# Folding two forward transforms and normalising rows block by block in a fused long-convolution and token-mixing kernel

## The chip, the cores and the metric

The kernel runs on one core of a Trainium2 chip. The metric is the device time of one execution in microseconds (us); lower is better. "Span" is the time from the first to the last instruction in the profile; in these kernels the device time is the span plus about 1.8 to 2.4 us. TensorE multiplies matrices, VectorE (DVE in the profile), ScalarE (ACT) and GpSimd (POOL) do the rest, SyncE (SP) issues most transfers. GpSimd issues the others, in particular those that add to their destination.

## The reference, cut to what matters

```python
def _A_ref(q, k, v, shift_k, ssm_k, ssm_D):          # S = 2048 rows, D = 640
    k_shift = sum of 4 shifted copies of k, each times a tap of shift_k
    kv = k_shift * v
    y  = irfft(rfft(kv, 4096) * rfft(ssm_k, 4096))[:2048]     # long convolution
    return q * (y + kv * ssm_D)

def _B_ref(x, w1, b1, w2, b2):
    h = layernorm(x)                                  # over D
    return w2^T @ gelu(w1^T @ h + b1) + b2            # mixes the S rows

x = A_q;  g = sigmoid((x * gate_w).sum(-1))
result = g * _A_ref(x, ...) + (1 - g) * _B_ref(x, ...)        # as the kernel combines them
```

The kernel does the Fourier transforms as matrix products with sine tables (`FTB` forward, `GTB` inverse). There are two pairs of forward transforms: of the filter (`wT`, two halves) and of `kv` (`vkv0` and `kv1`). Between transforms VectorE runs "mixings", additions and subtractions that combine four partial spectra.

## The kernel before

The kernel holds its own list scheduler. It gives every operation an assumed duration, simulates the engines, and emits each engine's instructions in the order that this simulation found. Semaphore waits are then added from real data dependencies.

```python
def dma(o, i, nbytes, stream="SP", prio=None, sem=None, rate=320.0, chain=False, **kw):
    ...  # the scheduler assumes nbytes / rate for a transfer

def k_turn(hk):                       # one block of keys: a copy on VectorE, then a transposing transfer
    o, i = kp[hk % 2], kn[hk % 2]
    ...  # VectorE copy kp <- kn
    dma(KT[hk // 2][:, :, c0:c0 + 128], o[:, :, :], 128 * 5120, rate=170.0, transpose=True, chain=True)

def ln_apply():                       # after the statistics of all 16 row tiles
    ts("POOL", sd[:, :], mv[:, :, 1], 1e-5, None, ALU.add)
    tt("POOL", rstd[:, :], sd[:, :], V(cst, 1, [[0, 16]]), ALU.pow)
    tt("POOL", sd[:, :], sd[:, :], rstd[:, :], ALU.mult)
    for t in range(16):
        ...  # VectorE: X[t] = (X[t] - mean) * rstd

def v1mix(Wh, Ws, Vh, Vs):            # two transfers that ADD reversed spectra to their destination
    for i in range(2):
        dma(V(Vh, ...), V(Wh, ...), 128 * 5120 * 2, stream="POOL", prio=0, accum=True)
v1mix(C[0], 2, C[1], 2)
v1mix(SS, 0, C[0], 0)
```

`KT` (transposed keys) feeds the shift products on TensorE, which give `ksh`. VectorE multiplies that with `v` into `vkv`, and the transform of `vkv` follows.

Of the kernel before, what the change touches and what calls it, by code (L numbers as in the profile page):

```python
# [11 lines left out]
I32 = mybir.dt.int32  # L12
ACT = mybir.ActivationFunctionType
# [5 lines left out]
class _Tracker:  # L19
# [31 lines left out]
    def regions(self, ap):  # L51
# [10 lines left out]
        pstride, pcount = apl[0]  # L62
        if pcount > 1:
            assert pstride == rowsize, (name, apl, rowsize)
        p0 = off // rowsize
# [187 lines left out]
    def dma(self, stream, out_ap, in_ap, semname, transpose=False, noncontig=False, accum=False):  # L253
        reads = [in_ap] + ([out_ap] if accum else [])
        writes = [out_ap]
        acc = self.pre(stream, reads, writes)
        engobj = self.eng[stream]
        sem = self.dma_sems[semname]
        if transpose:
            ins = engobj.dma_start_transpose(out_ap, in_ap)  # L260
        elif accum:
            ins = engobj.dma_start(out_ap, in_ap, accum_op=ALU.add, max_dma_last_dim=2560)  # L262
        elif noncontig:
            with self.nc.allow_non_contiguous_dma(reason="tiny"):
                ins = engobj.dma_start(out_ap, in_ap)
        else:
            ins = engobj.dma_start(out_ap, in_ap)  # L267
        ins.then_inc(sem, 16)
        self.dma_cnt[semname] += 16
        v = self.dma_cnt[semname]  # L270
        self.dma_hist[(semname, v)] = dict(self.known[stream])
        src = ("dma", semname, v)
        for reg, mode in acc:
            self.add_record(reg, mode, src)
        return v
# [229 lines left out]
def _build(nc, A_q, A_k, A_v, A_shift_k, A_ssm_k, A_ssm_D, B_x, B_w1, B_b1, B_w2, B_b2, gate_w, out):  # L505
# [10 lines left out]
    with ExitStack() as es:  # L516
# [38 lines left out]
        cw = alloc("cw", [128, NG, 7], BF16)  # L555
        m32 = alloc("m32", [128, 32], BF16)
        cc = alloc("cc", [128, 28], F32)
        stats = alloc("stats", [128, 16, 12], F32)
# [11 lines left out]
        FTB = alloc("FTB", [128, 4, 2, 2, 2, 128], BF16)  # L570
# [7 lines left out]
        acol = alloc("acol", [128, 2, 4], I32, at=base_of(SS))  # L578
        brow = alloc("brow", [128, 2, 128], I32, at=base_of(SS) + 64)
        dif = alloc("dif", [128, 128], I32, at=base_of(SS) + 64 + 1024)  # L580
        dif2 = alloc("dif2", [128, 32], I32, at=base_of(SS) + 64 + 1536)
        KT = [alloc(f"KT{i}", [128, NG, KTW], BF16) for i in range(2)]
        gq = [alloc(f"gq{i}", [128, 2, D], BF16, at=base_of(GTB) + 2560 * i) for i in range(3)]
        ssm = alloc("ssm", [128, ND, S], BF16, at=base_of(C[3]))
        wT = alloc("wT", [128, 4, 4, D], BF16, at=base_of(C[2]))
# [7 lines left out]
        pint = alloc("pint", [128, 4, 2, 2, 256], I32, at=base_of(ring[1]))  # L593
# [88 lines left out]
        def dma(o, i, nbytes, stream="SP", prio=None, sem=None, rate=320.0, chain=False, **kw):  # L682
# [5 lines left out]
            rd = [i] + ([o] if kw.get("accum") else [])  # L688
# [19 lines left out]
        def ssm_load(hk):  # L708
            dma(ssm[:, :, 512 * hk:512 * hk + 512], dr(A_ssm_k, 512 * hk, [[S, 128], [128 * S, ND], [1, 512]]), 128 * ND * 1024, chain=True)
# [4 lines left out]
        def w1_load(c, hk):  # L714
            dma(ring[c % 2][:, 4 * hk:4 * hk + 4, :], dr(B_w1, 512 * hk * F + 512 * c, [[4 * F, 128], [F, 4], [1, 512]]), 128 * 4096, chain=True)

        def k_load(hk):
            dma(kn[hk % 2][:, :, :], dr(A_k, 512 * hk * D, [[4 * D, 128], [1, 4 * D]]), 128 * 5120, chain=True)

        def k_turn(hk):  # L720
# [4 lines left out]
            c0 = 16 + 128 * (hk % 2)  # L725
            dma(KT[hk // 2][:, :, c0:c0 + 128], o[:, :, :], 128 * 5120, rate=170.0, transpose=True, chain=True)

        def v_load(hk):
            dst = vkv0[:, hk, :, :] if hk < 2 else v1[:, hk - 2, :, :]
            dma(dst, dr(A_v, 512 * hk * D, [[4 * D, 128], [1, 4 * D]]), 128 * 5120, chain=True)  # L730
# [8 lines left out]
        for hk in range(2):  # L739
            ssm_load(hk)  # L740
# [5 lines left out]
        dma(gwb[:, :], dr(gate_w, 0, [[0, 128], [1, D]]), 128 * 1280, chain=True)  # L746
        for hk in range(1, 4):
            x_load(hk)
        ssm_load(2)
        ssm_load(3)  # L750

# [5 lines left out]
        iota(acol[:, :, :], [[512, 2], [1, 4]], 0, 4)  # L757
        iota(brow[:, :, :], [[2, 2], [4, 128]], 1, 0)
        iota(dif2[:, :], [[1, 32]], 128, -1)
        ts("DVE", ident[:, :], dif[:, :], 0.0, None, ALU.is_equal)  # L760
        memset("POOL", cw[:, :, :], 0.0)
        ro, ri = rows[0:20, 3, :].rearrange("g (j q c) -> g j q c", j=4, q=4), V(rows, 0, [[1, 4], [0, 4], [4, 32]], pn=20)
        SC.add("POOL", 1.3, lambda s: T.op("POOL", lambda e: e.tensor_copy(ro, ri), [ri], [ro]), [ri], [ro], name="taps")
        PORD = (0, 2, 1, 3)
        for p in PORD:
            pv = pint[:, p, :, 1, :]
            tt("DVE", pv, V(acol, p, [[4, 2], [0, 256]]), V(brow, 0, [[0, 2], [1, 256]]), ALU.mult, mode=1)
            ts("DVE", pint[:, p, :, 0, :], pv, 1024.0, None, ALU.add, mode=2)
            pa = pint[:, p, :, :, :].rearrange("q a b c -> q (a b c)")
            ts("DVE", pa, pa, 4095, None, ALU.bitwise_and, mode=2)  # L770
            act(FTB[:, p, :, :, :, :].rearrange("q a b c d -> q (a b c d)"), pa, ACT.Sin, bias=cst[:, 0:1],
                scale=-(2.0 * math.pi / 4096.0) * (1.0 - 1e-6), name="sin")

        for hk in range(2):
            k_load(hk)
        for hk in range(4):
            w1_load(0, hk)

# [15 lines left out]
        def transp(h, p, kt):  # L794
            vt = _VT("cv")
            items = []
            hk = 2 * h + kt
            dfold = hk == 0 and p == 0
# [3 lines left out]
            for db in range(ND):  # L802
                items.append(((lambda s, db=db: s[:, db * 128:db * 128 + 128]),
                              V(ssm, db * S + 512 * hk + p, [[4, 128]]), ident[:, :], not dfold, True))
            mms(vt, items, name="wtr")
            act(wT[:, hk, p, :], full, ACT.Copy, vt=vt, name="wT")

        def fwd(src, h, p, dst, slot, scale, name, neg=lambda c, k2: False):
            for k2 in range(2):
                for c in range(2):  # L810
                    vt = _VT("cv")
                    items = []
                    for kt in range(2):
                        for ci in range(2):
                            items.append((chk(ci), FTB[:, p, kt, c, k2, :], src(kt, p, ci), kt == 0, kt == 1))
                    mms(vt, items, name=name)
                    o = dst[:, slot, 2 * c + k2, :].rearrange("p (a b) -> p a b", a=2)
                    sc = -scale if neg(c, k2) else scale
                    kw = {} if sc == 1.0 else {"scale": sc}
                    act(o, two, ACT.Copy, vt=vt, name=name + "e", **kw)  # L820

        def mixing(R, Th, Ts, fine=False, conj=False):
            def sl(h, s, n=1):
                return V(h, s * SL, [[1, n * SL]])
# [3 lines left out]
            for i, n in (((0, 1), (1, 1)) if fine else ((0, 2),)):  # L828
                tt("DVE", sl(Th, Ts + i, n), sl(R, i, n), sl(R, 2 + i, n), ALU.add)
                tt("DVE", sl(R, i, n), sl(R, i, n), sl(R, 2 + i, n), ALU.subtract)  # L830
            tt("DVE", sl(R, 2), sl(Th, Ts), sl(Th, Ts + 1), ALU.add)
            tt("DVE", sl(R, 3), sl(Th, Ts), sl(Th, Ts + 1), ALU.subtract)
# [16 lines left out]
        def ln_apply():  # L849
            ts("POOL", sd[:, :], mv[:, :, 1], 1e-5, None, ALU.add)  # L850
            tt("POOL", rstd[:, :], sd[:, :], V(cst, 1, [[0, 16]]), ALU.pow)
            tt("POOL", sd[:, :], sd[:, :], rstd[:, :], ALU.mult)
            for t in range(16):
# [3 lines left out]
        srcW = lambda h: (lambda kt, p, ci: wT[:, 2 * h + kt, p, 320 * ci:320 * ci + 320])  # L857
        for h in range(2):
            for p in PORD:
                for kt in range(2):  # L860
                    transp(h, p, kt)
            for p in PORD:
                fwd(srcW(h), h, p, C[h], p, 1.0 / 1024.0, "W", (lambda c, k2: k2 == 1) if h == 0 else (lambda c, k2: c == 1))
            if h == 0:
# [3 lines left out]
                ln_apply()  # L868
                for g0 in (0, 10):
                    tt("POOL", KF[:, g0:g0 + 10, :, :], V(cw, 7 * g0, [[7, 10], [1, 7], [0, 32]]), V(m32, 0, [[0, 10], [0, 7], [1, 32]]), ALU.mult)  # L870
                for hk in range(2):
                    k_turn(hk)
                mixing(C[0], SS, 0, fine=True)
            else:
                mixing(C[1], C[0], 0, conj=True)

        memset("POOL", KT[0][:, :, 15:16], 0.0)
        for hk in range(2):
            v_load(hk)
        for hk in range(2, 4):  # L880
            k_load(hk)
        for hk in range(2, 4):
            v_load(hk)
        for hk in range(2, 4):
            k_turn(hk)
        for hk in range(4):
            w1_load(1, hk)

        def v1mix(Wh, Ws, Vh, Vs):
            for i in range(2):  # L890
                dma(V(Vh, (Vs + i) * SL, [[1280, 2], [1, 1280]]), V(Wh, (Ws + i) * SL + 1280, [[-1280, 2], [1, 1280]]),
                    128 * 5120 * 2, stream="POOL", prio=0, accum=True)

        v1mix(C[0], 2, C[1], 2)
        v1mix(SS, 0, C[0], 0)

        def kv(hk):
            h, kt = hk // 2, hk % 2
            kb = ksh[hk % 2]
            for g0, ng in ((0, 8), (8, 8), (16, 4)):  # L900
                vt = _VT("cv")
                items = []
                for b in range(ng):
                    g = g0 + b
                    c0 = 16 + 128 * kt
                    items.append(((lambda s, b=b: s[:, 128 * b:128 * b + 128]), KT[h][:, g, c0:c0 + 128],
                                  KF[:, g, 0:4, :].rearrange("p a b -> p (a b)"), True, False))
                    items.append(((lambda s, b=b: s[:, 128 * b:128 * b + 96]), KT[h][:, g, c0 - 1:c0 + 127],
# [244 lines left out]
```

## Time and profile before

| | before |
|---|---|
| device time, median | 192.68 us (192.67 to 192.70) |
| span | 190.9 us |
| TensorE busy | 177.4 us (93%) |
| VectorE busy | 170.3 us (89%) |
| first forward transform of the filter / of kv starts | 14.29 / 50.28 us |

The next lines are from the page of the kernel before: busy time by engine, and TensorE's busy share and granted clock, in tenths, in 40 slices of the span.

```profile
PE 177.4 (93%) x1403; PEld 130.5 (68%) x1403; DVE 170.3 (89%) x195; ACT 116.4 (61%) x187; POOL 33.0 (17%) x29
...
PE   0749989999799999999999999999999999999993
...
PEclk9999999999999999999999999999999999999999
```

TensorE works almost without a break after the first quarter. (The trace's records of the granted clock begin at 16.3 us in this run, so the 9s of `PEclk` before that say nothing.) To see how much it loses even while "busy", I took the start of every matmul from the trace and subtracted from each interval what that matmul takes when nothing holds it: 0.1357 us for 320 columns, 0.0557 us for 128 and 0.0425 us for 96, the spacings of its unhindered stretches. The remainder is lost time. By this estimate, the kernel before has 169.1 us of matmul work and loses 18.6 us: 12.5 us by 17.1 us, 5.2 us from there to 62 us, and 0.8 us after that.

This is the timeline of SyncE's queue in the kernel before (start, length of the issue, source line, transfer, count):

```profile
22.42 10.61 SPq L260 DMA_TRANSPOSE KT<-kp  x2
...
48.19 6.34 SPq L260 DMA_TRANSPOSE KT<-kp  x2
```

And this is GpSimd's timeline, with the adding transfers:

```profile
57.02 2.64 POOL L262 DMA_DIRECT2D C<-C  x2 [19.65 <-DVE C L617]
61.34 2.43 POOL L262 DMA_DIRECT2D C<-SS  x2 [1.68 <-DVE C L617]
```

From the view of the tile `KT` in the kernel before, the time from issue to landing of the four transposes:

```profile
DMA to landing us min/median/max: 4.9/5.0/9.7
```

The last transpose is issued at 51.35 us and has landed by 56.3 us. The adding transfers begin at 57.02 us. The two kinds do not meet, but nothing in the program sees to that.

### The profile page before, as it was taken

To read this page: it belongs to the slowest core of one execution; us is meant where nothing else is said; L and a number is where in the kernel's file an instruction comes from. 1 tells how busy PE (TensorE), PEld (TensorE's weight loads), DVE (VectorE), ACT (ScalarE), POOL (GpSimd) and SP (SyncE) were. 2 spreads that over 40 slices of the span, in tenths; PEclk is the share of its full clock that TensorE was granted. 3 is DMA by queue.
4 is the path that set the end of the run, shared out by engine and by line. 5 is a ranking of instruction groups with operands and counts; after the bars stand their busy time and mean duration, and the time that the engine had idled before them with its cause. 6 is when DMAs were issued, how large, how long until landed. Compare 5 with 4: busy or idle time off the path is not lost.

```text
span 190.9 us, 3358 instructions
## 1 busy us (share of the span) xinstructions
PE 177.4 (93%) x1403; PEld 130.5 (68%) x1403; DVE 170.3 (89%) x195; ACT 116.4 (61%) x187; POOL 33.0 (17%) x29
## 2 busy tenths in 40 slices
PE   0749989999799999999999999999999999999993
PEld 0536555678566976767777777888888777886782
DVE  7999967999999799999999969999999958999451
ACT  4799997889599999998411221131322467516632
POOL 2619563600006300010012102250000000000000
PEclk9999999999999999999999999999999999999999
DMA  5999999993799999994368914999947903210222
GB/s 155 327 412 378 372 238 230 307 407 136 136 181 306 250 232 306 272 329 96 59 138 251 231 27 138 272 208 195 263 136 224 367 18 137 72 69 2 72 103 103
DMA packets 37296, 38.93 MB, mean 204 GB/s; under 512 B 15644, under 2 KB 32673, under 8 KB 37281
## 3 DMA queue, kind: packets, MB, share of 16 engines
q1 hardware_dynamic: 34464, 32.15, 54.7%
q0 software_dynamic: 2752, 6.55, 18.6%
q8 instruction: 11, 0.18, 0.4%
q14 instruction: 5, 0.03, 0.0%
q10 hardware_dynamic: 64, 0.01, 0.0%
HBM read 25.87 MB, written 2.62 MB: 149 GB/s over the span
## 4 chain that ended last, share of the span: by engine, by line
PE 71%; DVE 19%; DMA 4%; POOL 2%; issue 2%; SPq 0%; ACT 0%; DVEq 0%
PE pp L293 71%; DVE stats L845 6%; DMA X<-in_A_q_dram 4%; DVE X L628 3%; DVE SS L617 3%; DVE C L617 2%; DVE kp L724 2%; POOL rstd L617 2%; DVE vkv L617 1%; DVE mv L847 1%; POOL sd L627 1%; SPq L267 0%; ACT O L655 0%; DVE O L617 0%; DVEq L187 0%
## 5 line engine op out<-in xcount | busy, mean ns | idle before, releaser
L293 PE MATMUL pp<-X,ring 128*128 128x320 bf16 x384 | 54.0, 299 | 0.1
L293 PE MATMUL pp<-GT,W 128*128 128x320 bf16 x384 | 52.8, 299 | 0.0
L617 DVE TENSOR_TENSOR C<-C 128x2560 bf16<-128x2560 bf16 (+1 forms) x28 | 48.9, 1769 | 1.2 <-ACT C L655 1.1
L293 PEld LDWEIGHTS pp<-GT,W 128*128 128x128 bf16 x384 | 43.5, 113 | 8.9 <-ACT cgb L655 0.2
L293 PEld LDWEIGHTS pp<-X,ring 128*128 128x128 bf16 x384 | 37.1, 98 | 15.4 <-DVE X L628 0.7
L655 ACT ACTIVATE C<-pp 128x640 bf16<-128x640 f32 x64 | 39.6, 741 | 4.4 <-PE pp L293 4.3
L655 ACT ACTIVATE O<-pp,c,omg 128x640 bf16<-128x640 f32 (+1 forms) x17 | 14.5, 853 | 32.9 <-PE pp L293 32.9
L655 ACT ACTIVATE GT<-pp,cc 128x640 bf16<-128x640 f32 x12 | 9.6, 797 | 22.1 <-PE pp L293 21.9
L617 DVE TENSOR_TENSOR tm<-C,C 128x2560 bf16<-128x2560 bf16 (+2 forms) x12 | 20.2, 1708 | 1.9 <-DMA C<-tm 1.9
L293 PE MATMUL pp<-wT,FTB 128*128 128x320 bf16 x128 | 19.6, 310 | 0.6 <-ACT wT L655 0.4
L655 ACT ACTIVATE cgb<-pp,gg 128x640 bf16<-128x640 f32 x16 | 12.7, 793 | 7.7 <-PE pp L293 7.7
L293 PEld LDWEIGHTS pp<-wT,FTB 128*128 128x128 bf16 x128 | 11.5, 101 | 8.0 <-ACT C L655 2.3
L617 DVE TENSOR_TENSOR C<-tm 128x2560 bf16<-128x2560 bf16 (+1 forms) x12 | 15.0, 1263 | 0.1
L293 PE MATMUL pp<-ident,ssm 128*128 128x128 bf16 x80 | 8.8, 265 | 6.6 <-DMA ssm<-in_A_ssm_k_dram 5.3
L262 POOL DMA_DIRECT2D C<-C x6 | 7.5, 1407 | 36.0 <-DVE C L617 36.0
L845 DVE BATCH_NORM_STATS2 stats<-X 128x6 f32<-128x320 bf16 x32 | 13.4, 463 | 0.3 <-DMA X<-in_A_q_dram 0.3
L293 PE MATMUL pp<-C,GTB 128*128 128x320 bf16 x96 | 13.6, 299 | 0.0
L293 PEld LDWEIGHTS pp<-ident,ssm 128*128 128x128 bf16 x80 | 6.3, 127 | 9.1 <-DMA ssm<-in_A_ssm_k_dram 5.3
L293 PEld LDWEIGHTS pp<-C,GTB 128*128 128x128 bf16 x96 | 9.0, 98 | 4.0 <-ACT O L655 0.2
L655 ACT ACTIVATE gq<-gq 128x640 bf16<-128x640 bf16 x16 | 11.8, 756 | 0.0
L617 DVE TENSOR_TENSOR tm<-C,SS 128x5120 bf16<-128x5120 bf16 x4 | 11.2, 2817 | 0.0
L655 ACT ACTIVATE wT<-pp 128x640 bf16<-128x640 f32 x16 | 10.1, 812 | 1.1 <-PE pp L293 1.1
(64 smaller groups left out, 177.2 us busy)
## 6 DMA issues: line engine op xcount, KB each, us to landing
ring<-in_B_w_dram SPq DMA_DIRECT2D x12, 512.0 KB, 10.3
W<-in_B_w_dram SPq DMA_DIRECT2D x8, 768.0 KB, 7.3
C<-C POOLq DMA_DIRECT2D x6, 640.0 KB, 10.5
ssm<-in_A_ssm_k_dram SPq DMA_DIRECT2D x4, 640.0 KB, 9.1
X<-in_A_q_dram SPq DMA_DIRECT2D x4, 640.0 KB, 9.5
kn<-in_A_k_dram SPq DMA_DIRECT2D x4, 640.0 KB, 9.2
out_dram<-O SPq DMA_DIRECT2D x7, 320.0 KB, 2.3
vkv<-in_A_v_dram SPq DMA_DIRECT2D x2, 640.0 KB, 4.7
```

The costliest lines, as they stand in the source:

```text
L262: ins = engobj.dma_start(out_ap, in_ap, accum_op=ALU.add, max_dma_last_dim=2560)
L293: ins = self.nc.tensor.matmul(ps_ap, lhsT=lhsT, rhs=rhs, start=start, stop=stop, skip_group_check=True)
L617: return SC.add(eng, d, lambda s: T.op(eng, lambda e: e.tensor_tensor(o, a, b, op), [a, b], [o]), [a, b], [o], prio=prio, name="tt")
L627: return e.tensor_scalar(o, a, s1, None, op0=op0)
L628: return e.tensor_scalar(o, a, s1, s2, op0=op0, op1=op1)
L655: return T.op("ACT", lambda e: e.activation(o, src, func, **kw), rr + [src], ww)
L724: SC.add("DVE", 0.75, lambda s: T.op("DVE", lambda e: e.tensor_copy(ov, iv), [i[:, :, :]], [o[:, :, :]]), [i[:, :, :]], [o[:, :, :]], prio ...
L845: SC.add("DVE", 0.38, (lambda o, i: lambda s: T.op("DVE", lambda e: e.bn_stats(o, i), [i], [o]))(o, i), [i], [o])
L847: SC.add("DVE", 0.12, (lambda o, i: lambda s: T.op("DVE", lambda e: e.bn_aggr(o, i), [i], [o]))(o, i), [i], [o])
```

## The change

The intent: use the symmetry of the transforms (row n and row N-n) to fold the inputs, so that the forward transforms need 224 matmuls instead of 256 and each mixing two wide VectorE operations fewer. Rows are normalised per block of 512 so that token mixing can start early. GpSimd builds the shift table in five pieces between the blocks. Key loads move up. The reversed blocks come by indirect loads from GpSimd, and the inverse table is computed with sines on ScalarE instead of by transposing transfers. The core of the diff (cuts are marked with `...`):

```diff
-        def ln_apply():
-            ts("POOL", sd[:, :], mv[:, :, 1], 1e-5, None, ALU.add)
-            tt("POOL", rstd[:, :], sd[:, :], V(cst, 1, [[0, 16]]), ALU.pow)
...
+        def ln_scale(hk):
+            a, b = 4 * hk, 4 * hk + 4
+            ts("POOL", sd[:, a:b], mv[:, a:b, 1], 1e-5, None, ALU.add, prio=0)
+            tt("POOL", rstd[:, a:b], sd[:, a:b], V(cst, 1, [[0, 4]]), ALU.pow, prio=0)
+            return tt("POOL", sd[:, a:b], sd[:, a:b], rstd[:, a:b], ALU.mult, prio=0)
...
+        def turn(h, d0, nd, eng="POOL"):          # reversed copy of filter columns
+            o, i = ssmR[h][:, d0:d0 + nd, :, :], V(ssm, ..., [[1024, nd], [1, 4], [-4, 128]])
...
         def transp(h, w):                          # a transpose, or two that add or subtract (fold)
+                items.append((..., col(db, e, p), ident[:, :], not dfold, e2 is None))
+                if e2 is not None:
+                    items.append((..., col(db, e2, p2), (nident if ng else ident)[:, :], False, True))
...
-                for g0 in (0, 10):
-                    tt("POOL", KF[:, g0:g0 + 10, :, :], ...)
+        for n_, g0 in enumerate((0, 4, 8, 12, 16)):
+            tt("POOL", KF[:, g0:g0 + 4, :, :], ...).after.update((turn1, lnl[1 + n_ // 2]))
...
-        for hk in range(2, 4):
-            k_turn(hk)
+        k_load(3)
+        kturns = [k_turn(hk) for hk in range(2, 4)]
...
+        kturns += [w1_load(1, hk) for hk in range(4)]
         def v1mix(Wh, Ws, Vh, Vs):
...
-                    128 * 5120 * 2, stream="POOL", prio=0, accum=True)
+                    128 * 5120 * 2, stream="POOL", prio=0, accum=True).after.update(kturns)
```

`.after` orders the adding transfers behind the key transposes in the scheduler's simulation.

## The prediction

> **What bounds it now.** The page gives TensorE 177.4 us busy of a 190.9 us span. The chain of waits reads DMA of A_q, then layernorm statistics, one VectorE mixing step, POOL `sd`/`rstd` (25.6 to 30.0) and sixteen row scalings until 35.8, a few more VectorE links, then TensorE alone from 51.75 to 187.83. In stretches, TensorE is unbroken from 51.75 on; its real stalls lie earlier: 5.3 us for the first load, about 6 us between 5.3 and 14.3 (40 transposes of 64 ns paced by evacuations), about 6 us more to 51.75. VectorE is nearly co-critical: it works almost without gaps until its last mixing ends at 174.7, and TensorE takes the last inverse transform 0.9 us later.
>
> **TensorE work.** Folding drops 32 of 256 forward matmuls of 320 columns: 32 x 0.1365 us (256 in 34.9 us) = -4.4 us. The folded weights need 140 transposes instead of 80: +60 x 0.064 = +3.9 us. Net -0.5 us; the folding as such buys TensorE nothing. Evacuations stay 80.
>
> **VectorE work.** Each of four mixings loses two 2560-wide operations: -8 x 1.41 = -11.3 us. Added: two folds of about 2.25 us, a reversed copy of 0.8 to 1.7, the inverse table computed instead of transposed by DMA (about +6.2, from 0.36 us per 512 and 0.62 us per 1024 integers). Smaller forward table: about -1. Net about zero, so VectorE stays near 165 us before the last inverse.
>
> **What moves.** Rows are scaled per block, so I expect the first block ready near 17 to 19 us, against 30.5. By the instruction order, 120 token-mixing matmuls come before the first forward transform of kv, against 58, filling the evacuation-paced stretches. In exchange the second row of transposes must wait for the reversed copy on VectorE and POOL, so steady work starts near 10 us (before, the first transposes ran at 5.3 but stalled).
>
> POOL now carries copies, descriptor issues, four `pow` groups and five table pieces in order. In before, `sd` (0.2 us of work by its sibling) took 1.4 us, ending 0.1 us after a VectorE two-input operation did; that agrees with the Trainium skill, "SBUF — State Buffer", section "Who interferes with whom": a VectorE instruction with two SBUF inputs contends with a GpSimd instruction that reads SBUF. I expect waits of 0 to 3 us in row scaling from this and from the late first key block.
>
> ScalarE gains at least eight table loads (1.28 us each) between gelu and sine, in the 3.5 us gaps it has there: harmless.
>
> **Sum.** TensorE: start 10 + about 170.5 of work + 2 stalls + 3 tail = 185.5 to 186.5 of span. VectorE: mixing of the first kv transform starts near 61.5 (63.6 before), 108 us of work to the last mixing, 3 to 5 idle, then 14 on TensorE: 187 to 188. Device time is the span + 1.8. I predict **188.0 us**, 80% range **184.8 to 191.2**; chances: faster by over 2% 0.55, within 2% 0.42, slower 0.03. The gain is removed early stalls, not removed work.
>
> **What would show it.** TensorE busy nearly unchanged (176 to 179); VectorE busy within 3 us of 170; first block's token-mixing matmuls near 20 us; first kv transform near 56 us, with 120 token-mixing matmuls done; in the chain, POOL `rstd` gone as one 3 us link; `ssmR` copies or their load as the early link; SS of the last mixing near 173 us.
>
> **What would make it wrong.** The reversed copies or `pow` on POOL several us slower than their size suggests, starving scaling (slower); the four-column `pow` costing as much as the sixteen-column one (2.9 us); the indirect loads arriving late; or the late VectorE chain stalling less than I count (then 185).

## More of the kernel before

The buffer `kp1` shares memory with `gq`, a scratch buffer of the gate.

## The result, and the profile after

The changed kernel takes **212.26 us** (median of 4 runs, 211.88 to 212.57) against 192.69 us for the kernel before on the same chip. The ratio is 1.101 (95% interval 1.0995 to 1.1033). A ratio here is the mean time of one kernel's fast runs over the mean of the other's in the same rounds, so it is not quite the ratio of the medians.

The same lines of the page, for the changed kernel:

```profile
PE 178.1 (85%) x1431; PEld 131.2 (62%) x1431; DVE 179.6 (86%) x234; ACT 130.9 (62%) x198; POOL 44.2 (21%) x54
...
PE   1199999699994005979999999999999999999994
...
PEclk9999999999999755999999999999999999999999
```

TensorE's busy time has hardly moved. There is a hole of about three slices (5.25 us each), and the granted clock falls in it. The chain of waits by line, from the same page, names a cause:

```profile
PE pp L296 52%; DMA KT<-kp 12%; DVE stats L896 6%; DVE X L640 6%; ACT C L667 4%; DVE C L629 3%; DVE pint L640 2%; ACT gq L667 2%; ACT ksh L667 2%; DVE kp L746 1%; DVE SS L629 1%; DVE mv L898 1%; DVE ssmR L828 1%; DVE gq L629 1%; DVE pint L639 1%
```

12% of the span, 25.6 us, is one key transpose. These are the table of waits and the view of the tile `KT` for the changed kernel:

```profile
POOL KT L954 <- DMA KT<-kp: 18.1, 1, 18.1
DVE gq L629 <- DMA KT<-kp: 16.7, 1, 16.7
...
PE pp L296 <- DVE vkv L629: 15.7, 1, 15.7
```

```profile
DMA to landing us min/median/max: 6.3/7.4/25.6
```

VectorE stands 16.7 us because `gq` may overwrite `kp1` only when the last transpose has read it. Behind it, in order, stands the folding of `vkv`, for which TensorE stands 15.7 us. The timeline of VectorE in the changed kernel shows the queue:

```profile
52.77 0.82 DVE L746 COPY kp<-kn 128x2560 bf16<-128x2560 bf16 x1
...
61.37 1.16 DVE L629 TENSOR_TENSOR ux<-vkv 128x1920 bf16<-128x1920 bf16 x1
79.25 0.82 DVE L629 TENSOR_TENSOR gq<-X,gwb 128x1280 bf16<-128x1280 bf16 x1 [16.72 <-DMA KT<-kp]
79.99 1.26 DVE L629 TENSOR_TENSOR vkv<-vkv 128x1280 bf16<-128x1280 bf16 x2
```

The last key copy ends at 53.6 us, and its transpose is issued at once. GpSimd's timeline of the changed kernel shows what is issued in the same microseconds:

```profile
53.16 1.33 POOL L265 DMA_DIRECT2D C<-C  x1 [3.86 <-DVE C L629]
55.30 1.20 POOL L265 DMA_DIRECT2D C<-C  x1 [0.81 <-DVE C L629]
58.83 2.41 POOL L265 DMA_DIRECT2D C<-SS  x2 [2.33 <-DVE C L629]
79.38 1.58 POOL L954 COPY KT<-KT 128x20 bf16<-128x20 bf16 x2 [18.14 <-DMA KT<-kp]
```

The adding transfers, which came after the transposes in the kernel before, now run beside the last one. The trace's packet records, counted in bins of 2 us, show what that does (changed kernel, all 16 DMA engines together; the bins from 52 to 56 us, where the third transpose ends, are left out):

```
us        transpose packets (256 B)    adding packets (2560 B)
50-52           1665                        0
56-58            497                       51
58-60             70                       53
60-62            262                       48
62-64            125                       71
64-66            110                       92
66-68             72                       60
68-70             89                       92
70-72            114                      104
72-74            162                      131
74-76            205                      111
76-78             98                       86
```

Alone, the transpose moves 1665 packets in 2 us; a packet takes 18 ns (median). Beside the adding transfers it moves 70 to 262 from 58 us on, in most bins about one for each packet of the other kind, and an adding packet takes 214 ns (median). A transpose has 2560 such packets, so one for one against 214 ns is a very bad deal. The Trainium skill ("DMA: Bandwidth & Descriptors", section "Queues, rings and completion order") says that each DMA engine goes round robin between its queues and changes after a whole packet. The counts of most bins agree, if a record of the trace is what the page calls a packet. But turns alone are not the whole price: with 214 and 31 ns (the median of a transpose packet here), 16 engines could move about 130 of each kind in 2 us by an estimate, which only the bin from 72 us reaches. The adding transfers suffer too: in the kernel before they moved 155 to 162 packets in 2 us from 64 to 70 us. What else slows both is not shown.

This is the table of stretches around the hole in the changed kernel (bounds, length, then busy time of each engine with its instructions, clock, DMA share, GB/s):

```profile
55.00:65.30 10.30, 10.12 (x108) 7.49 (x104) 7.50 (x6) 8.96 (x16) 3.61 (x3) 1.00 1.25 112
65.30:80.90 15.60, 0.01 (x1) 0.02 (x2) 1.65 (x3) 1.03 (x2) 1.46 (x2) 0.66 1.12 181
80.90:95.00 14.10, 13.04 (x132) 9.43 (x133) 12.73 (x11) 12.73 (x21) 0.06 (x1) 0.89 1.02 332
```

For 15.6 us almost nothing computes while the DMA engines are full (a share over 1 comes from packet records that overlap). After it, TensorE's matmuls start 0.267 us apart until 84.5 us and then 0.136 us apart. The Trainium skill ("TensorE: Matmul & The Clock Gate", section "What's actually happening") says that the array falls to half its clock when idle and needs about 3.4 us of work to get it back. That agrees with the 3.6 us here. By an estimate (half of these 3.6 us) the hole costs about 2 us on top of its length.

That explains some 16 to 18 of the 19.6 us lost against the kernel before. My first theory is therefore: **the collision of the adding transfers with a late key transpose costs about 16 us, and nothing else in the change costs much.** The rivals are that the aliasing of `gq` and `kp1` is to blame, or the adding as such, or some other part of the order.

### The profile page after: what moved, and what is told of

Read it like the earlier page. It is cut to its first block, busy times and chain, and to the rows that moved or that the text cites. A ratio compares the mean times of both kernels' runs of the same rounds, so it can differ in the third digit from the quotient of the medians.

```text
span 210.0 us, 3492 instructions
## 1 busy us (share of the span) xinstructions
PE 178.1 (85%) x1431; PEld 131.2 (62%) x1431; DVE 179.6 (86%) x234; ACT 130.9 (62%) x198; POOL 44.2 (21%) x54
## 4 chain that ended last, share of the span: by engine, by line
PE 52%; DVE 24%; DMA 12%; ACT 9%; issue 2%; POOL 0%; POOLq 0%
PE pp L296 52%; DMA KT<-kp 12%; DVE stats L896 6%; DVE X L640 6%; ACT C L667 4%; DVE C L629 3%; DVE pint L640 2%; ACT gq L667 2%; ACT ksh L667 2%; DVE kp L746 1%; DVE SS L629 1%; DVE mv L898 1%; DVE ssmR L828 1%; DVE gq L629 1%; DVE pint L639 1%
## 5 line engine op out<-in xcount | busy, mean ns | idle before, releaser
L296 PE MATMUL pp<-X,ring 128*128 128x320 bf16 x384 | 55.4, 299 | 2.8 <-DVE X L640 1.5
L667 ACT ACTIVATE C<-pp 128x640 bf16<-128x640 f32 x64 | 40.2, 730 | 18.5 <-PE pp L296 18.2
L296 PEld LDWEIGHTS pp<-X,ring 128*128 128x128 bf16 x384 | 36.5, 98 | 19.5 <-DVE X L640 3.6
L629 DVE TENSOR_TENSOR C<-C 128x2560 bf16<-128x2560 bf16 x21 | 30.9, 1485 | 1.1 <-ACT C L667 1.0
L629 DVE TENSOR_TENSOR gq<-X,gwb 128x1280 bf16<-128x1280 bf16 x8 | 6.6, 821 | 16.7 <-DMA KT<-kp 16.7
L296 PE MATMUL pp<-vkv,FTB 128*128 128x320 bf16 x36 | 6.0, 318 | 15.7 <-DVE vkv L629 15.7
L296 PE MATMUL pp<-wT,FTB 128*128 128x320 bf16 x112 | 17.2, 300 | 0.3 <-ACT C L667 0.3
L667 ACT ACTIVATE cgb<-pp,gg 128x640 bf16<-128x640 f32 x16 | 12.7, 792 | 4.5 <-PE pp L296 4.5
L629 DVE TENSOR_TENSOR C<-C,C 128x2560 bf16<-128x2560 bf16 (+1 forms) x12 | 15.0, 1264 | 0.3 <-ACT C L667 0.3
L296 PEld LDWEIGHTS pp<-vkv,FTB 128*128 128x128 bf16 x36 | 3.5, 103 | 17.8 <-DVE vkv L629 16.0
L296 PEld LDWEIGHTS pp<-wT,FTB 128*128 128x128 bf16 x112 | 9.9, 98 | 6.3 <-ACT C L667 2.0
```

Of the source, the lines that this page charges most:

```text
L296: ins = self.nc.tensor.matmul(ps_ap, lhsT=lhsT, rhs=rhs, start=start, stop=stop, skip_group_check=True)
L629: return SC.add(eng, d, lambda s: T.op(eng, lambda e: e.tensor_tensor(o, a, b, op), [a, b], [o]), [a, b], [o], prio=prio, name="tt")
L667: return T.op("ACT", lambda e: e.activation(o, src, func, **kw), rr + [src], ww)
```

## The experiments

### Is it the collision?

**a1_acc_waits**: the adding transfers really wait for the transposes. (`hold` names the half of `KT` that the third and fourth transposes write; the first two have landed by 47.4 us.)

```diff
-    stream="POOL", prio=0, accum=True).after.update(kturns)
+    stream="POOL", prio=0, accum=True, hold=<KT[1]>).after.update(kturns)
```

> The changed kernel, same instruction order, but the four accumulating transfers (C<-C, C<-SS, issued by POOL) wait until all four key transposes KT<-kp have landed. Theory A (the accumulating transfers share the DMA rings with the last transpose and slow it from about 5 to 25.6 us): the last transpose lands within 8 us of its issue, the 16.7 us VectorE wait and the 15.7 us TensorE wait vanish, time 192 to 196 us. Rival B (the last transpose is slow by itself because it is issued late behind other loads): its landing stays above 15 us and the time stays above 205.

Measured: 196.29 us (196.27 to 196.47), ratio 1.0186 to the kernel before (1.0169 to 1.0203). This is 0.3 us above my band. 16.0 us are back with the same order of instructions. The view of the tile `KT`, and a line of the table of waits:

```profile
DMA to landing us min/median/max: 4.9/6.2/8.1
```

```profile
POOL C L267 <- DMA KT<-kp: 9.8, 1, 9.8
```

The wait is now GpSimd's: 9.8 us before the adding transfers, and no wait in this run's table ends with their landing. The collision is the cause of 16 us. VectorE's timelines show where they went: this is the start of the mixing of the first kv transform in the kernel before, the changed kernel and a1_acc_waits, one fence each.

```profile
63.57 2.83 DVE L617 TENSOR_TENSOR C<-C 128x5120 bf16<-128x5120 bf16 x1 [1.06 <-ACT C L655]
```

```profile
82.97 1.49 DVE L629 TENSOR_TENSOR C<-C 128x2560 bf16<-128x2560 bf16 x1 [0.99 <-ACT C L667]
```

```profile
67.55 3.02 DVE L631 TENSOR_TENSOR C<-C 128x2560 bf16<-128x2560 bf16 x2 [2.38 <-ACT C L669]
```

**a2_plain_copy**: the same transfers as plain copies, a wrong result.

```diff
-    stream="POOL", prio=0, accum=True).after.update(kturns)
+    stream="POOL", prio=0, accum=False).after.update(kturns)
```

> The changed kernel with the four accumulating transfers replaced by plain copies of the same shape from the same POOL queue (wrong result on purpose). If any large POOL-queue transfer beside the transpose does it by taking turns packet by packet, the transpose stays slow (landing 12 us or more) and the time above 200 us[...]. If it is the accumulation as such, the transpose lands in under 9 us and the time is 192 to 196.

Measured: 196.44 us, ratio 1.0191; transposes land in 6.0/7.6/9.0 us. The result still passed the comparison, so its tolerance does not see these terms. Plain copies of the same size do little harm. In the trace they move 512 packets of 5120 B at about 206 ns, where the adding form moves 1024 packets at 214 ns, so they hold the engines half as long, and the transposes run in the pauses between them: 1150 and 1344 transpose packets in the two bins from 56 to 60 us, where only 34 and 7 of the copies moved, but 107 against 94 from 54 to 56 us. By my two branches this points to the adding (the time is 0.4 us above that band); the one-for-one turns show in both forms. It would be wrong to conclude that only adding transfers do this; r3_all below shows a plain load that did.

**a3_gq_later**: take away the aliasing as the first wait, by ordering the gate products that use `kp1`'s memory behind the last kv product.

```diff
-    tt("DVE", gb[:, :, :], X[...], V(gwb, ...), ALU.mult)
+    tt("DVE", gb[:, :, :], X[...], V(gwb, ...), ALU.mult).after.add(<last kv product>)  # gq0 and gq1 only
```

> The changed kernel with the gate products that write the buffers in which the transposed keys lie (gq 0 and 1) ordered after the last key-times-value product. Rival C (the wait is made by buffer reuse: VectorE stops at gq only because the buffer is still being read): time falls by 12 us or more, to under 200. Theory A: the late transpose also holds the second half's key filter, so the wait moves to TensorE at KF,KT, and only the work that can pass it (about 40 forward matmuls and some mixing, 4 to 8 us) is won: 204 to 208.

Measured: 206.05 us (205.65 and 206.46), ratio 1.069. The last transpose still took 25.3 us; the wait only moved to those who need the keys themselves (ScalarE's `ksh` 9.4 us, TensorE 8.6 us behind GpSimd's `KT` copies). The aliasing brought the wait forward by some 6 us, but it is not the cause of the rest.

**b1_before_collide**: the kernel before, with its last key copy put late, so that the collision happens there.

```diff
-    r3: tt("DVE", sl(R, 3), ..., ALU.subtract)   # in the second mixing
-    for hk in range(2, 4): k_turn(hk)
+    k_turn(2);  k_turn(3) ordered after r3
```

> The kernel before, with only the VectorE copy of the last key block ordered later, after the mixing step that releases the accumulating transfers, so that the last key transpose meets them. Theory A: the last transpose takes 15 us or more to land instead of 5, TensorE stalls, time 203 to 213 us. Rival B (it has to do with the folded kernel's other loads): the transpose lands in under 9 us and the time is 192 to 196.

Measured: 205.97 us (205.26 and 206.68), ratio 1.0686. The view of the tile `KT`, and a line of the table of waits, for this run:

```profile
DMA to landing us min/median/max: 4.9/7.1/22.8
```

```profile
PE pp L293 <- DMA KT<-kp: 11.7, 1, 11.7
```

The old kernel without any of the change's parts loses 13.2 us when its order lets the two meet. The later issue (58.17 instead of 51.35 us) does not explain it: a landing in 4.9 us would have been at 63.1 us (an estimate), and TensorE stopped for this transpose only at 69.3 us.

**r1_rate**: no wait at all, but one number changed in the scheduler of the changed kernel. The page of the changed kernel shows 365 to 398 GB/s in the slices from 5 to 26 us (and 109 in the next), while the scheduler assumes 320.

```diff
-    def dma(..., rate=320.0, ...)
+    def dma(..., rate=400.0, ...)
```

> The changed kernel with one number altered: the transfer rate that its own ordering assumes, 400 instead of 320 GB/s[...]. No wait is added. The order then puts the key copies some 5 us earlier (the last one about 3 us earlier), so the key transposes should be issued before or just as the accumulating transfers start. First theory: the slowest transpose lands within 13 us instead of 25.6, and the time falls from 212.3 us to 193 to 200 us. Rival (something else in the order costs the 16 us): 208 us or more.

Measured: 195.06 us (three runs 194.97 to 195.08 and one of 197.25), ratio 1.016 (1.0099 to 1.022). Its order issues the last transpose at 52.3 us and the first adding transfer at 53.95 us:

```profile
DMA to landing us min/median/max: 5.6/6.9/8.2
```

A change of one assumption is worth 17 us here. With it the last transpose is issued 1.35 us earlier, and ahead of the adding transfers.

**b2_before_rate**: the control for that, the same number in the kernel before.

> Control: the kernel before with the same altered number (400 instead of 320 GB/s in its own ordering). Theory: nothing collides there either way, 191.7 to 193.7 us. If the number were a gain in itself, by several us: 190 us or less, and r1_rate's 17 us would not all belong to the collision.

Measured: 199.61 us (199.23 to 200.49), ratio 1.0356. My expectation (191.7 to 193.7) failed: the number makes the kernel before slower by 6.8 us. No transpose collided with the adding transfers (max 7.1 us). The order now put the first key copy ahead of its data; VectorE stood 2.35 us for it and the copy took 3.75 us, the row scalings came later, and TensorE stood 3.00 us for a scaled row at 33.2 us. After that its granted clock was 0.50 from 34.4 to 41.2 us, by an estimate 2.5 us of the loss (half of the 4.97 us that it worked there). So the number is no gain in itself, which leaves the collision as the reason for r1_rate's 17 us; r2_rate_wait below, the same order with the real wait, takes as long as r1_rate (195.13 us). It also shows how fragile an order is that rests on assumed arrivals.

### What of the remaining 3.6 us?

a1_acc_waits is still 1.9% slower than the kernel before. The lost-time estimate described above shows where. Each row closes: work, lost time and a tail of 3.3 us after the last matmul add up to the span within 0.1 us.

```
lost time of TensorE, us   to 17.1   17.1-30   30-62   62-100   later    sum    matmul work
before                       12.5       3.1      2.1      0.4     0.4    18.6      169.1
changed                      12.7       1.6      3.2     19.8     1.2    38.6      168.1
a1_acc_waits                 12.7       1.6      3.2      4.7     0.5    22.8      168.1
r1_rate                      12.5       1.6      6.0      1.2     0.3    21.6      168.1
r2_rate_wait                 11.7       2.1      6.1      1.2     0.3    21.5      168.1
v1_spread                    10.9       1.6      3.6      5.1     0.5    21.7      168.1
s3_keys                      12.7       1.3      4.4      1.2     0.3    19.9      168.1
s1_spread                    11.1       4.5      3.5      1.0     0.3    20.5      168.1
s5_key_early                 11.6       1.7      3.3      2.5     0.5    19.5      168.1
```

Two things stand out. The whole folding saves TensorE 1.0 us of work (an estimate from counts and spacings: 32 matmuls of 0.1357 us less, 60 transposes of 0.0557 us more). And a1_acc_waits loses 4.2 us more than the kernel before, mostly from 62 to 100 us. The theories were: GpSimd's work beside VectorE's row scalings; the late start of the second phase; and the row blocks themselves.

**u1_norm_once**: a1_acc_waits with the row blocks undone.

```diff
-    ts/tt("POOL", sd/rstd[:, a:b], ...) per block, ln_apply(hk - 1) after each
+    a, b = 0, 16: one ln_scale after the statistics of all blocks, then ln_apply(0..3)
```

> The changed kernel with its accumulating transfers held back (196.3 us), and the row-block normalisation undone: one power over 16 columns after the statistics of all four blocks, as in the kernel before. Second theory (what is left of the loss sits in the first 17 us: the reversed copies and the slow doubled transposes): row blocks are worth under 1 us either way, 195.3 to 197.3 us. Rival (the row blocks themselves cost the rest, by the small GpSimd steps between them): 192.5 to 194.5 us. If the row blocks bring what my prediction said: 198 us or more.

Measured: 199.65 us (198.55 to 200.69), ratio 1.0371: the third branch, slower than a1_acc_waits by 3.4 us. **u2_before_rows** is the other half, the kernel before with row blocks only (and the table in five pieces):

> The kernel before, with the row-block normalisation alone (four powers of 4 columns, the shift table in five pieces). Before, TensorE stood still for only 2.1 us in all after its 9.47th us up to the end of the kernel that lay outside the wait for the first ScalarE copies, so there is little to win: second theory 191.7 to 193.7 us. If row blocks bring what my prediction said: under 191 us. If GpSimd's pieces beside VectorE's scalings cost more than the earlier start wins: over 194 us.

Measured: 192.67 us (192.56 to 192.72), ratio 0.9996 (0.9979 to 1.0013). So undoing the row blocks costs 3.4 us in the changed kernel, and putting them in brings nothing in the old one. The reason is in u1's VectorE timeline, where the first scaling comes at 37 us; in the kernel before it came at 30.05 us.

```profile
37.04 2.58 DVE L642 TENSOR_SCALAR X<-X,mv,rstd 128x640 bf16<-128x640 bf16 x7 [2.84 <-POOL rstd L631]
```

TensorE stands 3.0 us for it at 34.6 us, and then its granted clock was 0.50 from 37.9 to 41.3 us, by an estimate another 1.7 us (half of that stretch). GpSimd's work has pushed the `sd` and `rstd` steps back: all five table pieces ran from 20.92 to 29.19 us, one VectorE mixing operation beside them took 5.26 us instead of the 1.48 us of the kernel before, so the last statistics came at 30.46 us, and an indirect load stood between `sd` and `rstd`. The row blocks avoid this damage from the rest of the change. But u1's edit also dropped the order between table pieces and blocks, so the 3.4 us are not shown to be the row blocks' alone.

**p1_pool_quiet**: GpSimd's table pieces and second reversed copy cut to a seventh and an eighth (wrong result; the missing parts are zeroed by VectorE at the start).

```diff
-    tt("POOL", KF[:, g0:g0 + 4, :, :], ...)          # 7 x 32 elements for each of 4 groups
+    tt("POOL", KF[:, g0:g0 + 4, 0:1, :], ...)        # 1 x 32
-    turn on GpSimd: 128 columns
+    turn on GpSimd: 16 columns
+    memset("DVE", KF, 0); memset("DVE", ssmR[1], 0)
```

> The changed kernel with its accumulating transfers held back (196.3 us), and GpSimd's shift-table pieces and second reversed copy cut to a seventh and an eighth of their elements (wrong result on purpose; the missing elements are zeroed at the start). Second theory, GpSimd part: VectorE's row scalings fall from 4.05, 1.69 and 3.48 us to about 1.1, 0.5 and 1.6, TensorE's 1.54 us wait for a scaled row goes, and the time falls by 1 to 2 us, to 194.3 to 195.5. Rival (these waits are hidden, the loss is all at the start): 195.8 to 196.8 us.

Measured: 198.14 us, ratio 1.0275, slower, and inconclusive for the time: the two zeroings took VectorE 3.05 us and moved the first reversed copy from 8.82 to 11.90 us, so everything started 3.1 us later. But the durations answer the question about the scalings. These are the group of row scalings in the list of groups (busy time, mean ns, idle before) for the kernel before, a1_acc_waits and p1_pool_quiet, one fence each:

```profile
L628 DVE TENSOR_SCALAR X<-X,mv,rstd 128x640 bf16<-128x640 bf16 x16 | 5.8, 438 | 3.2 <-POOL rstd L617 3.2
```

```profile
L642 DVE TENSOR_SCALAR X<-X,mv,rstd 128x640 bf16<-128x640 bf16 x16 | 13.0, 854 | 0.0
```

```profile
L642 DVE TENSOR_SCALAR X<-X,mv,rstd 128x640 bf16<-128x640 bf16 x16 | 6.6, 452 | 0.6 <-POOL rstd L631 0.6
```

The same sixteen operations take 13.0 us beside GpSimd's work and 6.6 us without most of it. Four of them make the difference: in a1_acc_waits they took 3.39, 1.69, 1.01 and 2.41 us, and each ended 0.2 us after the GpSimd copy or table piece beside it, while the other twelve took 0.39 to 0.48 us. This is the contention that the Trainium skill ("SBUF — State Buffer", section "Who interferes with whom") gives for a `tensor_scalar` in a fast mode: whoever issues first holds the shared ports for the whole instruction. The trace agrees with the blocking. It shows neither the mode nor who came first: the scaling of 3.39 us is recorded from 18.45 us, the first copy beside it from 19.02 us, and starts on GpSimd are rough. What it costs the kernel stays below that: with a 3.1 us later start p1 ended only 1.9 us later, so some 1.2 us by an estimate from these two numbers.

**v1_spread**: a1_acc_waits with the first reversed copy ahead of the last table rows, the second half's filter load and copy earlier, and the last table piece placed after the last row scaling.

```diff
+    ssm_load(1, 1)            # moved ahead of w1_load(0, 0)
-    ... name="turn")
+    ... prio=0, name="turn")
-    .after.update((turn1, lnl[1 + n_ // 2]))
+    .after.update((turn1, lnx if n_ == 4 else lnl[1 + n_ // 2]))     # lnx: last row scaling
```

> The changed kernel with its accumulating transfers held back (196.3 us), the first half's reversed copy put ahead of the last twelve table rows on VectorE, the second half's load and reversed copy earlier, and the last piece of the shift table after the last row scaling. Second theory: the first reversed copy starts near 5.5 us instead of 8.8, the forward transforms start 1.5 to 3 us earlier than 17.07, TensorE's wait at 37 us goes, and the time is 192.0 to 194.3 us. Rival (the start is hidden behind later work on ScalarE or VectorE): 195.3 to 196.8 us.

Measured: 195.30 us (195.28 to 195.39), ratio 1.0134: 1.0 us better, less than expected. The forward transforms started at 14.61 instead of 17.07 us. But the last table piece ran from 35.14 to 36.84 us, still beside the last scalings (3.79 us for four), because the order was made for assumed times; TensorE's wait there became 1.74 us instead of 1.54. And 5.1 us were still lost from 62 to 100 us.

**g1_gate_late**: the gate's products and sums of three row blocks taken out of the stretch from 75 to 90 us, where ScalarE is nearly full (14.6 of 15 us in a1_acc_waits).

```diff
-    if ft in (1, 3, 5, 7): gate work of block ft // 2
+    if ft in (1, 7, 8, 9): gate work of block max(ft - 6, 0), ordered after that gelu
```

> The changed kernel with held-back accumulating transfers (196.3 us), and the gate's products and sums over three of the four row blocks taken out of the stretch from 75 to 90 us and put behind the second key-times-value transform. Theory that ScalarE paces TensorE there: TensorE's loss between 62 and 90 us falls from 4.7 us to 3 us or less and the time to 193.8 to 195.5 us. Rival (TensorE waits for VectorE there, or the work only moves): 195.8 to 197.5 us.

Measured: 197.60 us, ratio 1.0256: slower, 0.1 us beyond the rival's band. The loss from 62 to 90 us fell only from 4.7 to 3.8 us, and 2.3 us more were lost after 100 us, where TensorE had been unbroken. The rival is right: the work only moved.

**r2_rate_wait**: earlier keys (400 GB/s assumed) and the real wait together.

> The same with the accumulating transfers held back too. Theory for the last 3.5 us: the first key-times-value transform starts too late (61.2 us against 50.3 before), so that both such transforms, the shift products and the gate sums fall into one stretch where ScalarE is full and TensorE loses 4.7 us between 62 and 90 us. With earlier keys the transform starts near 55 us, TensorE loses under 2.5 us there, and the time is 192.5 to 194.8 us. Rival (it is the doubled transposes at the start): 195.8 to 196.8 us.

Measured: 195.13 us (195.09 to 195.25), ratio 1.0129, just outside my band. The mechanism was as expected from 62 to 100 us: the loss fell from 4.7 to 1.2 us, with the first kv transform at 58.2 instead of 61.2 us. But the loss from 30 to 62 us rose from 3.2 to 6.1 us. VectorE now stood 2.0 us for the first key block, with row scalings behind it.

**r3_all**: earlier keys, the wait, v1_spread's moves, and 30 matmuls without a use before the first transposes.

> Earlier keys, held-back transfers, the earlier reversed copies and later last table piece of v1_spread, and 30 idle-time matmuls before the first transposes, so that these run at the 56 ns of later ones and not at 107 ns. If each part pays by itself: 190.0 to 192.3 us, under the kernel before. If the first transposes are paced by ScalarE and not by TensorE, the extra matmuls bring nothing: 191.5 to 193.5 us.

Measured: 202.29 us (201.16 to 203.38), ratio 1.0479, the worst of this series. The tile `KT` and VectorE's timeline say why:

```profile
DMA to landing us min/median/max: 4.9/7.2/20.8
```

```profile
59.25 0.83 DVE L748 COPY kp<-kn 128x2560 bf16<-128x2560 bf16 x1 [7.31 <-DMA kn<-in_A_k_dram,bidx]
```

Here the third transpose ran beside an indirect load issued by GpSimd (5120-B packets). From 46 to 56 us the transpose moved 165 to 434 packets in 2 us and the load 11 to 36. Both starved. So the collision is not peculiar to adding transfers. But with about 5 to 24 transpose packets for one of the load these are not the one-for-one turns of the changed kernel, and why both starved is not shown. TensorE then stood 5.7 us from 57.3 us, and its granted clock was 0.50 from 34.7 to 38.1 and from 62.0 to 68.8 us.

**s3_keys**: r2_rate_wait with the first key block loaded ahead of the last block of weights, and the third transpose held until the fourth key block has landed.

```diff
-    w1_load(0, 1..3); k_load(0)
+    w1_load(0, 1..2); k_load(0); w1_load(0, 3)
-    dma(KT..., transpose=True, chain=True)
+    dma(KT..., transpose=True, chain=True, hold=kn[1] if hk == 2 else None)
```

> The kernel of r2_rate_wait (195.13 us) with the first key block loaded ahead of the last block of weights, and the third key transpose held until the fourth key block has landed. If VectorE's 2.0 us wait for the first key block is what delays the row scalings: TensorE's waits of 1.45 and 0.65 us at 32 to 35 us go and the time is 192.7 to 194.2 us. If GpSimd's pieces delay them: 194.6 to 195.8 us.

Measured: 193.64 us (193.52 to 193.75), ratio 1.0046 (1.003 to 1.0063), as the first branch said. TensorE's waits of 1.45 and 0.65 us at 32 to 35 us are gone. All transposes landed within 5.7 us.

**s1_spread** is s3_keys with v1_spread's three moves:

> s3_keys with the first reversed copy before the last twelve table rows, the second half's load and reversed copy earlier, and the last table piece after the last row scaling. v1_spread won 1.0 us with these three. If that adds to the earlier keys: 1 us or more below s3_keys, 191.5 to 193.2 us. If TensorE only waits elsewhere: within 0.5 us of s3_keys.

Measured: 193.25 us (192.32 to 194.12), ratio 1.0008 (0.9983 to 1.0034): within 0.4 us of s3_keys. The earlier start is there (11.1 us lost by 17.1 us, not 12.7), but VectorE paid it back at once:

```profile
27.38 0.83 DVE L748 COPY kp<-kn 128x2560 bf16<-128x2560 bf16 x1 [4.48 <-DMA kn<-in_A_k_dram]
```

**s2_spread_warm** is s1_spread with 30 matmuls without a use while TensorE is idle:

```diff
+    mms(<spare PSUM slot>, 30 x (ident @ ident), prio=0)
```

> s1_spread with 30 matmuls without a use while TensorE is idle at the start. If the half-rate transposes (107 instead of 56 ns each until about 15 us) pace the start: 0.5 to 1.5 us below s1_spread. If ScalarE's copies (0.6 us for each of the eight) pace it: within 0.3 us of s1_spread.

Measured: 194.91 us (194.41 to 195.70), ratio 1.0102: slower by 1.7 us, against both branches. The transposes ran 56 ns apart until 8.2 us, but 107 ns apart from there to 11.6 us: the granted clock, 1.00 before, was 0.50 in these 3.4 us, after TensorE had stood 2.1 us idle behind the extra matmuls. The first filter transform came only 0.4 us earlier (14.91 instead of 15.30 us). TensorE then stood 3.6 us for a scaled row at 26 us, and the granted clock was 0.50 again from 28.7 to 35.5 us. In s1_spread's profile, a wait of 2.28 us there was followed by 0.50 from 28.8 to 32.2 us only. By an estimate (half of the time that TensorE worked in them) these two stretches cost 2.9 and 1.7 us; with the longer wait, that accounts for the 1.6 us between the two profiled runs (195.70 and 194.12 us). So a wait of 2 to 4 us can cost TensorE nearly its length again; the same is seen in b2_before_rate, u1_norm_once and r3_all, and waits of 1.55 us in a1_acc_waits and 1.75 us in v1_spread were not followed by it.

**s4_key_after** and **s5_key_early** take s1_spread's 4.48 us wait away: both place the first key copy behind the second block's scalings, and s5 also loads that block one weight block earlier.

```diff
-    k_turn(0)
+    k_turn(0) ordered after the scalings of row block 1
-    w1_load(0, 1..2); k_load(0); w1_load(0, 3)        # s5 only
+    w1_load(0, 1); k_load(0); w1_load(0, 2..3)
```

> s1_spread with only the copy placed behind the second row block's scalings. TensorE's 2.29 us wait goes in part, but VectorE still stands 2 to 4 us for the block, now ahead of the third row block's statistics: 191.8 to 193.3 us.

> s1_spread with the first key block loaded one block of weights earlier still, and its copy placed behind the second row block's scalings. VectorE's 4.48 us wait and TensorE's 2.29 us wait for a scaled row should go: 190.5 to 192.3 us, under the kernel before (192.8). If the weights that now come later are missed, or the work only waits elsewhere: 192.7 to 194 us.

Measured: s4 194.87 us (194.38 to 195.45, ratio 1.0115), s5 193.31 us (193.16 to 193.36, ratio 1.0027, interval 1.0013 to 1.0041). In s5 the two waits went (VectorE stood 0.8 us for a later key block, TensorE not at all there), and a new wait of 1.26 us for GpSimd's `KT` copy appeared at 67 us; the 1.4 us for a gelu at 37 us is in s1_spread too. s4 missed its band by 1.6 us. Five orders of the same work (r2, s1, s3, s4, s5) thus gave medians of 193.3 to 195.1 us, and none beat 192.7.

What follows: with the collision removed and the order mended, the change brought nothing in the orders tried here. It saves 1.0 us of matmul work and loses at least about that much in waits (19.5 to 19.9 us against 18.6). I did not find a version that beats the kernel before; that none exists is not shown.

## Why the prediction was wrong, point by point

- **The result lies 24 us above the prediction and outside its range.** Sixteen of these are a transfer collision that the prediction did not contain at all. It named "the indirect loads arriving late" among the dangers, and in fact the last key block's indirect load was issued late (41.82 us, after a wait of 3.46 us) and its copy came at 52.77 us. But the step that failed is "VectorE: mixing of the first kv transform starts near 61.5". It started at 82.97 us, 21.5 us late, and in a1_acc_waits, without the collision, at 67.55 us: 15.4 us of the delay are the collision, and most of the other 6.1 us is the later first kv transform (61.15 us, said 56). The rest of that sum held: 111.8 us from there to the end of the last mixing (predicted 108 and 3 to 5 idle), then 15.2 us (predicted 14). The step treated transfers as free once issued. I read where the `.after` line put the adding transfers in the order, and did not ask what they would run beside. a1_acc_waits, b1_before_collide and r1_rate show the cause from three sides.
- **The sum for TensorE, without the collision, was 8 us too low.** It read "start 10 + about 170.5 of work + 2 stalls + 3 tail". In a1_acc_waits it is 12.7 us lost by 17.1 us, 168.1 of work, 10.1 us lost later, and a tail of 3.3 us: 194.2 us, for a span of 194.1. The term "2 stalls" was mis-sized by 8.1 us and "start 10" by 2.7 us, and 2.4 us less work gave a part back. "The gain is removed early stalls" fell with it: the early stalls were not removed. The early token-mixing matmuls filled some (3.1 to 1.6 us from 17 to 30 us), and others appeared later, for scaled rows, key products and ScalarE's copies.
- **"The folding as such buys TensorE nothing" was right**, at -0.5 us predicted and -1.0 us by the estimate. The 0.064 us assumed for a transpose was wrong, however: early on, in both kernels, they start 0.107 us apart and later 0.056 us. The Trainium skill ("TensorE: Matmul & The Clock Gate", section "What's actually happening") explains the two rates by the clock gate, and the trace agrees with both numbers.
- **VectorE "near 170" was wrong**: 179.6 us. Row scalings account for 7.2 us of the 9 (13.0 against 5.8 us). The prediction expected this contention, but cited the rule for two inputs, where the section's rule for fast modes fits a row scaling, and "0 to 3 us" of waits was too small. p1_pool_quiet shows 6.4 us of it to be GpSimd's.
- **Right as predicted:** TensorE's busy time (178.1, said 176 to 179); the first block's token mixing (21.1 us, said 20); 120 token-mixing matmuls ahead of the first kv transform; `rstd` no longer one link of 3 us (four columns took 1.05 us, so that danger did not come); a reversed copy as an early link of the chain.
- **The first kv transform** came at 61.2 us (said 56). The key copies ran at 32.6 to 52.8 us, later than the 21.6 to 49.5 us of before, although the change set out to move keys up: with 320 GB/s assumed, the order expected them later than they came.

## What to carry to other kernels

When a change moves a transfer, look at what else will be in flight on the same DMA engines in those microseconds. A transpose of many 256-B packets that landed in 4.9 us alone took 25.6 us beside adding packets of 2560 B and 20.8 us beside an indirect load of 5120-B packets (9.0 us beside plain copies in a2_plain_copy); if a later step depends on it, make the other transfer wait, not the order only. Do not count removed early waits as a gain before you have found which engine fills the space. Check every order that a scheduler made from assumed durations against the measured times, because one wrong assumption about arrivals moved this kernel by 17 us. When TensorE has waited 2 us or more, look at its granted clock after the wait as well.

## What the Trainium skill lacked or had wrong

- "DMA: Bandwidth & Descriptors", section "Rules for kernel authors": "A transpose next to ordinary DMAs needs nothing". That may hold for the result, but not for the time: beside adding transfers one transpose took 25.6 us to land where 4.9 to 8.1 us were measured in a1_acc_waits, which keeps them apart, and 20.8 us beside an indirect load.
- The same page, section "Queues, rings and completion order", says that engines change between queues after whole packets. That section gives no price of a packet by kind. Measured here: 18 ns for a 256-B transpose packet running alone, 214 ns for an adding packet of 2560 B, about 206 ns for a plain packet of 5120 B; so a plain copy held the engines half as long as an adding one of the same bytes.
- "SBUF — State Buffer", section "Who interferes with whom", gives the rule of contention, and a factor for each of two issue orders, but not what it costs a kernel. Here it was 6.4 us over sixteen row scalings (13.0 against 6.6 us) beside about 11 us of GpSimd copies and products.
- "TensorE: Matmul & The Clock Gate": the two spacings (107 and 56 ns) and the return to full rate after idling were confirmed (107, 56, and 3.6 us after the hole). Warming TensorE ahead with 30 matmuls did not hold here: after 2.1 us without work the granted clock fell to 0.50 and the transposes to 107 ns, from 8.2 to 11.6 us. What such a drop costs after a wait in mid-kernel was 1.7 to 2.9 us in u1_norm_once, b2_before_rate, s1_spread and s2_spread_warm, by estimate.
